# A gated FFN behind chunked attention: the zero columns beside h go, the centre tap comes first, and the hand-written order and engine tables are replaced

## The chip, the cores and the metric

The kernel runs on one core of one Trainium2 chip. The metric is device microseconds per execution, the median of three runs. The engines are written as in the profile: PE (TensorE, with PEld for its weight loads), DVE (VectorE), ACT (ScalarE), POOL (GpSimd) and SP (SyncE, which issues the DMAs here).

## The reference, cut to what matters

Chunked attention with 8 memory keys makes x (4 batches, 768 tokens, 512 channels). What the change touches is the second half:

```
h = relu(x @ w_in)                      # 768 tokens x 1024 channels, per batch
conv_out[t] = w0*h[t-1] + w1*h[t] + w2*h[t+1]    # per channel; h[-1] = h[768] = 0
out = (h * sigmoid(conv_out)) @ w_out   # 768 x 512
```

## The kernel before, in words

Channels lie on the 128 partitions and tokens along the free axis. h is made in 32 blocks: 4 batches of 8 channel blocks ("fc"), each 128 channels by 768 tokens, in two halves of 384 tokens. Attention is made in 32 pieces (batch, half, pair of heads).

Each float32 operand of a large product is split into a high and a low float32r part, and three products (high·high, high·low, low·high) replace one. The weights arrive as float64 words and are split on the chip by `from_f64`; one letter of W_IN, W_OUT, W_CONV for each block says how. For W_OUT, "C" scales the low part on ACT and multiplies on POOL, "M" does both in one DVE scalar_tensor_tensor; a lower-case letter puts the `max` of line 280 on POOL, not DVE.

One attention piece runs: scores on PE (L381), row maximum on DVE (L390), subtraction on DVE (L395) and one exp on ACT (L401) where SOFT has "V", or a small scaling on DVE (L407) and six exps with a bias on ACT (L413) where SOFT has "A"; row sum, reciprocal, normalisation (L427, on DVE or POOL by NORM), a transpose (TURN), the product with v on PE (L486), and the split of x into high (ACT, L489) and low (DVE, L492).

`ffn_in` makes one half of a block: 12 products on PE (L508) into one of four PSUM tiles "f", then the ReLU on ACT (L522) from "f" into h. h lives in a slot of the pool "u": 32 slots, 770 columns wide, which also hold x and the two parts of every gated block. Columns 0 and 769 of h must be zero for the convolution. The ReLU of the first half therefore issues a two-column memset on POOL (L521) ahead of itself, and waits for it.

`gated` then makes, for one block: the first tap (a scaling by a per-channel weight, on ACT, L534, or DVE, L538, by TAP), two scalar_tensor_tensor taps on DVE (L543), the sigmoid on ACT (L546), the multiplication by h (L550, on DVE or POOL by MULT; KEEP says whether the result goes over h or over the tap tile "w"), the high part (a copy on ACT, L554) and the low part (L557, on DVE or POOL by LO). `ffn_out` reads the parts of all 8 blocks of a batch: 24 products on PE (L569) for each 128 tokens. The last 128 tokens of batch 3 are done in two column halves.

The order is written out by hand. The program first lists 1529 operations (a product group, a ReLU, a tap and so on is one each), numbered as they are defined; `ORDER` then says in which order they are issued. Every engine executes its own operations in that order, one queue for each engine, and waits are made by what an operation reads and overwrites. Slots of a pool are handed out in that order as well: an operation that first writes a slot waits for the last readers of what was there.

Of the kernel before, what the change touches and what calls it, by code (L numbers as in the profile page):

```python
# [9 lines left out]
F32 = mybir.dt.float32  # L10
# [19 lines left out]
W_IN, W_OUT, W_CONV = "SMMSmMCM", "CMMMCMCM", "r"  # L30
TAP = "VAAAAAVAAAAAAAAAAAVVVVVAVVAAVAAA"
MULT = "VGGGGGGVGVGGGGGGVVGVGGGVGVGGVGGG"
LO = "VGGGVVGVGGGGVVGGVGVVGVGVVGVGVVVV"
SOFT = "AVVAAAAVVVAAVVVAVVVAVVVVVVAVVAVV"
NORM = "GGVVGVVGGGGGVGGGVVVGVVVVVGGGVGGV"
KEEP = "KKKKKNNKKKKKKNKKNKKNNKKNNNNNNKKK"
HOME = "wwwwwwwwwwwwwwwwwwwxwwwwwxxxwwxx"
# [158 lines left out]
def attention_then_gated_ffn(  # L196
# [302 lines left out]
    def ffn_in(b, fc, hf):  # L499
# [19 lines left out]
        def relu():  # L519
            if hf == 0:  # L520
                G.memset(h.t[:, 0 : S + 2 : S + 1], 0.0)  # L521
# [175 lines left out]
```

## Time and profile before

| | before |
|---|---|
| runs (three) | 366.35, 366.37, 367.98 us |
| median | 366.37 us |
| profiled execution, its own time | 366.92 us |
| its span, first to last instruction | 365.1 us |
| granted clock, mean | 0.995 |
| busy: PE, PEld, DVE, ACT, POOL | 339.9, 301.4, 252.0, 210.6, 104.6 us |

Busy times are those of the whole span. They average over stages with different limits, so the stages are read one by one below. Matmuls are pipelined, and a PE that is shown as busy can still be paced by others. POOL's spans are rough.

### The profile page before, as it was taken

What the parts mean: (1) busy time and instruction counts of PE and PEld (TensorE: products, weight loads), DVE (VectorE), ACT (ScalarE), POOL (GpSimd) and SP (SyncE); (2) the same over time, 40 slices, a digit from 0 to 9 for tenths busy, and PEclk for the clock granted to TensorE, in tenths of its full rate; (3) what the DMA queues carried; (4) which work ended last, traced back from release to release, by engine and by line L of the source; (5) the groups of instructions that cost most, each with busy time, mean ns of one, the idle gap of its engine ahead of it and who ended that gap; (6) DMA issues with size and microseconds to landing.
All of it is one profiled execution on the core that took longest, in us unless ns stands there. A gap on an engine that the chain in (4) does not pass through costs nothing.

```text
span 365.1 us, 7418 instructions
## 1 busy us (share of the span) xinstructions
PE 339.9 (93%) x2955; PEld 301.4 (83%) x2955; DVE 252.0 (69%) x429; ACT 210.6 (58%) x387; POOL 104.6 (29%) x114
## 2 busy tenths in 40 slices
PE   1799999899989988799999999899999999999996
PEld 1689899889979967779988789788998888888886
DVE  4999999999999999998999956230444991320000
ACT  2566879799889867857366795221566424420101
POOL 3314033284012353540316283400005615300000
PEclk9999999999999999899999999999999999999999
DMA  7997769467758372535054364411000102110102
GB/s 296 405 397 256 271 221 308 145 227 247 271 160 250 133 229 74 186 125 189 0 173 143 118 230 161 136 38 57 31 1 0 59 30 86 59 57 29 59 29 86
DMA packets 26386, 54.50 MB, mean 149 GB/s; under 512 B 3056, under 2 KB 13168, under 8 KB 26352
## 3 DMA queue, kind: packets, MB, share of 16 engines
q1 hardware_dynamic: 26352, 54.04, 42.6%
q8 instruction: 23, 0.38, 0.4%
q14 instruction: 11, 0.09, 0.1%
HBM read 44.79 MB, written 9.24 MB: 148 GB/s over the span
## 4 chain that ended last, share of the span: by engine, by line
PE 41%; DVE 21%; ACT 5%; issue 2%; DMA 1%; POOL 1%; SPq 0%; DVEq 0%; ACTq 0%; POOLq 0%
PE f L569 29%; PE f L508 10%; DVE w L543 9%; DVE w_top L293 2%; PE ta L486 1%; DVE e L427 1%; DVE z L422 1%; DVE u L492 1%; DVE top L390 1%; DVE u L557 1%; DMA w<-in_q_dram 1%; ACT u L522 1%; ACT e L413 1%; DVE w L457 1%; DVE e L395 1%
## 5 line engine op out<-in xcount | busy, mean ns | idle before, releaser
L508 PE MATMUL f<-u,w_in_hi 128*128 128x384 f32 x512 | 143.8, 347 | 6.2 <-ACT u L522 3.8
L569 PE MATMUL f<-w_out_hi,u 128*128 128x512 f32 (+1 forms) x400 | 125.2, 387 | 0.4 <-ACT w_top L580 0.4
L508 PEld LDWEIGHTS f<-u,w_in_hi 128*128 128x128 f32 x512 | 94.6, 190 | 10.4 <-ACT u L522 5.1
L569 PEld LDWEIGHTS f<-w_out_hi,u 128*128 128x128 f32 x400 | 74.1, 188 | 16.5 <-ACT w_top L580 0.8
L508 PE MATMUL f<-u,w_in_lo 128*128 128x384 f32 x256 | 87.2, 341 | 0.0
L543 DVE SCALAR_TENSOR_TENSOR w<-u,cw,w 128x768 f32<-128x768 f32 x64 | 78.1, 1231 | 4.4 <-ACT w L534 3.7
L569 PE MATMUL f<-w_out_lo,u 128*128 128x512 f32 (+1 forms) x200 | 77.1, 385 | 0.0
L522 ACT ACTIVATE u<-f 128x384 f32<-128x384 f32 x64 | 30.6, 493 | 35.1 <-PE f L508 27.7
L508 PEld LDWEIGHTS f<-u,w_in_lo 128*128 128x128 f32 x256 | 48.7, 190 | 0.6
L580 ACT COPY w_top<-f 128x512 f32<-128x512 f32 (+1 forms) x25 | 14.2, 572 | 59.8 <-PE f L569 54.0
L569 PEld LDWEIGHTS f<-w_out_lo,u 128*128 128x128 f32 x200 | 37.6, 188 | 7.2
L550 POOL TENSOR_TENSOR u<-w,u 128x768 f32<-128x768 f32 x16 | 28.9, 1810 | 41.5 <-ACT w L546 41.5
L546 ACT ACTIVATE w<-w 128x768 f32<-128x768 f32 x32 | 26.7, 845 | 15.8 <-DVE w L543 14.3
L486 PEld LDWEIGHTS ta<-a_d,w 128*64 128x64 f32 x768 | 26.1, 146 | 6.8 <-ACT a_d L446 3.3
L486 PE MATMUL ta<-a_d,w 128*64 128x64 f32 x768 | 28.9, 232 | 2.7 <-ACT a_d L446 1.8
L427 POOL TENSOR_TENSOR e<-e,z 128x384 f32<-128x384 f32 x17 | 16.1, 951 | 53.2 <-DVE z L424 46.6
L492 DVE TENSOR_TENSOR u<-ta,u 128x384 fp32r<-128x384 f32 x32 | 17.5, 548 | 12.8 <-ACT u L489 12.7
L381 PE MATMUL s<-k,w 128*64 128x64 f32 x672 | 24.8, 227 | 0.6 <-DVE e L395 0.6
L381 PEld LDWEIGHTS s<-k,w 128*64 128x64 f32 x672 | 22.1, 141 | 3.7 <-issue 2.0
L390 DVE TENSOR_REDUCE top<-s 128x6 f32<-128x384 f32 x32 | 17.2, 539 | 9.6 <-PE s L381 9.6
L557 DVE TENSOR_TENSOR u<-u,u 128x768 fp32r<-128x768 f32 x9 | 9.4, 1058 | 20.7 <-PE f L569 10.0
L557 POOL TENSOR_TENSOR u<-u,u 128x768 fp32r<-128x768 f32 x11 | 21.5, 1955 | 5.4 <-ACT u L554 3.5
(63 smaller groups left out, 373.7 us busy)
## 6 DMA issues: line engine op xcount, KB each, us to landing
w<-in_v_dram SPq DMA_DIRECT2D x32, 384.0 KB, 4.4
w<-in_q_dram SPq DMA_DIRECT2D x28, 384.0 KB, 4.3
k<-in_k_dram SPq DMA_DIRECT2D x28, 252.0 KB, 4.5
out_dram<-w_top SPq DMA_DIRECT2D x23, 256.0 KB, 2.0
w<-in_w_in_dram SPq DMA_DIRECT2D x8, 512.0 KB, 6.7
w<-in_w_out_dram SPq DMA_DIRECT2D x8, 512.0 KB, 4.6
t_dram<-w SPq DMA_DIRECT2D x15, 192.0 KB, 2.0
a_d<-t_dram SPq DMA_DIRECT2D x30, 96.0 KB, 2.5
```

What stands on the lines that cost most here:

```text
L381: nc.tensor.matmul(s.t[j * D : (j + 1) * D, o : o + KW], lhsT=q_[:, c], rhs=k_t.t[:, c * STEP : c * STEP + KW], start=True, stop=True,)
L390: lambda: V.tensor_reduce(out=pairs(top.t), in_=s_(), axis=AX.X, op=ALU.max), (s,), (top,),
L427: lambda: (V if norm == "V" else G).tensor_tensor(out=keys(e), in0=keys(e), in1=pairs(z.t).unsqueeze(3).broadcast_to([P, NG, 2, KW]), op=A ...
L486: nc.tensor.matmul(y, lhsT=v_g[:, g, u, h], rhs=a_d.t[:, :, o], start=True, stop=True)
L492: lambda: V.tensor_tensor(out=x.t[:, TW:S], in0=a.t[:, :TW], in1=x.t[:, :TW].bitcast(F32), op=ALU.subtract), (a, (x, 0)), ((x, 1),),
L508: nc.tensor.matmul(f.t[:, :TW], lhsT=w_in_p[c][:, fc, cc], rhs=x.t[:, a * TW : (a + 1) * TW], start=(cc == 0 and i == 0), stop=(cc == NCC ...
L522: A.activation(h.t[:, o : o + TW], f.t[:, :TW], AF.Relu)
L543: lambda j=j: V.scalar_tensor_tensor(out=c.t, in0=at(j), scalar=w[j], in1=c.t, op0=ALU.mult, op1=ALU.add),
L546: plan.op("A", act(S), lambda: A.activation(c.t, c.t, AF.Sigmoid), (c,), (c,), table="sigmoid")
L550: lambda: (V if mult == "V" else G).tensor_tensor(out=y_(), in0=c.t, in1=at(1), op=ALU.mult), (c, h), (y,), shared=True,
L557: lambda: (V if lo == "V" else G).tensor_tensor(out=g_lo(), in0=y_(), in1=g_hi().bitcast(F32), op=ALU.subtract),
L569: nc.tensor.matmul(ps.t[:, :n], lhsT=gs[b, fc][a].t[:, tt * P : (tt + 1) * P], rhs=w_out_p[c][:, fc, o : o + n], start=(fc == 0 and i == 0 ...
```

## The change

Four things change in the code.

- A "u" slot is 768 columns wide. h has no zero columns, and the ReLU issues no memset.
- The first tap is the centre one, over all 768 columns. The two outer taps are added over 767 columns each: the left one reads columns 0 to 766 of h and adds into columns 1 to 767 of the tap tile; the right one reads 1 to 767 and adds into 0 to 766. The count of instructions is the same.
- The engine tables and `ORDER` are new. Before to after, operations on DVE: TAP 10 to 5 of 32 (the rest on ACT), MULT 9 to 14, LO 17 to 17 with 12 blocks that trade places, SOFT "V" 21 to 19, NORM 15 to 16. For the weights of the output product one block goes from C to M (6) and one from M to m (1); the small conv weights go from r to R. KEEP trades four blocks, and HOME puts two more v tiles into another pool. TURN and W_IN are the same.
- Two cost figures that the order was planned with (`less=-15` lines, 75 to 185; -10 to -20) change; they issue nothing. The scratch for dynamic DMAs is 2048 bytes, before 1024.

```diff
-W_IN, W_OUT, W_CONV = "SMMSmMCM", "CMMMCMCM", "r"
-TAP = "VAAAAAVAAAAAAAAAAAVVVVVAVVAAVAAA"
-MULT = "VGGGGGGVGVGGGGGGVVGVGGGVGVGGVGGG"
-LO = "VGGGVVGVGGGGVVGGVGVVGVGVVGVGVVVV"
-SOFT = "AVVAAAAVVVAAVVVAVVVAVVVVVVAVVAVV"
-NORM = "GGVVGVVGGGGGVGGGVVVGVVVVVGGGVGGV"
-KEEP = "KKKKKNNKKKKKKNKKNKKNNKKNNNNNNKKK"
-HOME = "wwwwwwwwwwwwwwwwwwwxwwwwwxxxwwxx"
+W_IN, W_OUT, W_CONV = "SMMSmMCM", "CmMMCMMM", "R"
+TAP = "AAAAAAVAAAAAAAAAAVAVAVAAVAAAAAAA"
+MULT = "VGGVGGGGGVGGGGGGVVGVVVVVVGVGVVGG"
+LO = "VGGVVVVVVVGGGGVGVVVGGVGVVGGGGVVG"
+SOFT = "AVVAAAAVAVVAVVVAVVVAVVVVVVAAAVAV"
+NORM = "GGVVGGVGGGGGVGGGVVVGVVVVVGVGVVGV"
+KEEP = "KKKKKNNKKKKKKNKKNKKNNKKNKNKNNNNK"
+HOME = "wwwwwwwwwwwwwwwwwwxxwwwwwxxxwxxx"
 ORDER = [
...
-    plan.pool("u", [lambda t, i=i: work.tile([P, S + 2], t, name=f"u{i}", tag=f"u{i}", bufs=1) for i in range(NU)])
+    plan.pool("u", [lambda t, i=i: work.tile([P, S], t, name=f"u{i}", tag=f"u{i}", bufs=1) for i in range(NU)])
...
-        o = 1 + hf * TW
-
-        def relu():
-            if hf == 0:
-                G.memset(h.t[:, 0 : S + 2 : S + 1], 0.0)
-            A.activation(h.t[:, o : o + TW], f.t[:, :TW], AF.Relu)
-
-        plan.op("A", act(TW, True), relu, (f,), ((h, hf),))
+        plan.op(
+            "A", act(TW, True), lambda: A.activation(h.t[:, hf * TW : (hf + 1) * TW], f.t[:, :TW], AF.Relu), (f,), ((h, hf),)
+        )
...
-            plan.op("A", act(S, ptr=1), lambda: A.activation(c.t, at(0), AF.Copy, scale=w[0]), H, (c,))
+            plan.op("A", act(S, ptr=1), lambda: A.activation(c.t, h.t, AF.Copy, scale=w[1]), H, (c,))
...
-        for j in (1, 2):
+        for j, to, at in ((0, slice(1, S), slice(0, S - 1)), (2, slice(0, S - 1), slice(1, S))):
             plan.op(
                 "V", vec(S, 1, 1),
-                lambda j=j: V.scalar_tensor_tensor(out=c.t, in0=at(j), scalar=w[j], in1=c.t, op0=ALU.mult, op1=ALU.add),
-                (*H, c), (c,), shared=True,
+                lambda j=j, to=to, at=at: V.scalar_tensor_tensor(
+                    out=c.t[:, to], in0=h.t[:, at], scalar=w[j], in1=c.t[:, to], op0=ALU.mult, op1=ALU.add
+                ), (*H, c), (c,), shared=True,
             )
...
-    nc = _bacc.Bacc("TRN2", target_bir_lowering=False, num_devices=1, dynamic_dma_scratch_size=1024)
+    nc = _bacc.Bacc("TRN2", target_bir_lowering=False, num_devices=1, dynamic_dma_scratch_size=2048)
```

The new `ORDER` has 1528 entries, one less, since a C block has one operation more than an M block. Read as operations it is close to the old one: the same attention pieces and product groups come in nearly the same sequence on PE, and the activation tables are switched 20 times in both. Two places of it matter below:

| counted in `ORDER` | before | after |
|---|---|---|
| ahead of batch 3's first product group, on DVE: MULT, TAP, L395, L407 | 7, 7, 19, 10 | 8, 4, 17, 12 |
| there on DVE, weights: max of 512 columns, scalar_tensor_tensor, conv max | 15, 42, 0 | 14, 43, 1 |
| there on POOL: LO, MULT | 6, 16 | 4, 14 |
| there on ACT: taps | 17 | 20 |
| still to come on PE from there: L569 products, groups of L508, transposes | 414 + 48 half, 64, 0 | 417 + 48 half, 64, 1 |
| L569 products to come when batch 3's last block is first read | 108 + 48 half (fc 7) | 141 + 48 half (fc 7), 150 + 48 half (fc 4) |
| last low parts of batch 3 on the engine that makes them | fc 5, fc 7 on DVE | fc 3, fc 1, fc 4 on POOL, one after the other |

## Rows read from the trace of the kernel before

**Rows 1.** The page's busy times: us, share of the span, count.
```profile
PE 339.9 (93%) x2955; PEld 301.4 (83%) x2955; DVE 252.0 (69%) x429; ACT 210.6 (58%) x387; POOL 104.6 (29%) x114
```

**Rows 2.** Stages: length, busy us of PE, PEld, DVE, ACT, POOL, PEclk, DMA.
```profile
60.00:135.00 75.00, 70.28 (x815) 65.49 (x815) 72.94 (x122) 64.67 (x110) 25.77 (x26) 1.00 0.65 215
135.00:150.00 15.00, 11.34 (x110) 10.49 (x107) 14.67 (x23) 10.77 (x16) 5.21 (x6) 0.95 0.44 137
...
165.00:225.00 60.00, 59.65 (x550) 51.94 (x547) 53.50 (x84) 40.93 (x67) 23.26 (x13) 1.00 0.44 146
...
285.00:300.00 15.00, 15.00 (x66) 12.14 (x65) 14.96 (x13) 4.82 (x7) 6.10 (x3) 1.00 0.10 37
```

**Rows 3.** The chain that ended last, from 226 us: start, us, what.
```profile
228.12 1.61 POOL u L557
...
229.82 0.15 POOL u L521 x2
229.97 0.49 ACT u L522
...
230.50 5.01 PE f L508 x27
...
272.82 89.23 PE f L569 x408
```

**Rows 4.** PE's timeline, its longest wait after the start: [idle before <-releaser].
```profile
147.94 0.55 PE L439 MATMUL ta<-ident,e 128*128 128x128 f32 x3 [2.14 <-DVE e L427]
...
230.50 0.44 PE L508 MATMUL f<-u,w_in_hi 128*128 128x384 f32 x1 [1.59 <-ACT u L522]
```

**Rows 5.** The view of waits: us in total, times, longest.
```profile
ACT u L522 <- POOL u L521: 7.2, 5, 3.4
...
PE f L508 <- ACT u L522: 3.8, 4, 1.6
```

**Rows 6.** Groups by line: busy us, mean ns of one, idle before.
```profile
L543 DVE SCALAR_TENSOR_TENSOR w<-u,cw,w 128x768 f32<-128x768 f32 x64 | 78.1, 1231 | 4.4 <-ACT w L534 3.7
...
L550 POOL TENSOR_TENSOR u<-w,u 128x768 f32<-128x768 f32 x16 | 28.9, 1810 | 41.5 <-ACT w L546 41.5
...
L557 POOL TENSOR_TENSOR u<-u,u 128x768 fp32r<-128x768 f32 x11 | 21.5, 1955 | 5.4 <-ACT u L554 3.5 <-PE f L508 1.0 <-PE f L569 0.7
L534 ACT ACTIVATE w<-u,cw 128x768 f32<-128x768 f32 x22 | 20.7, 939 | 0.8 <-ACT u L489 0.3
...
L395 DVE TENSOR_TENSOR e<-s,top 128x384 f32<-128x384 f32 x21 | 11.5, 551 | 0.3
L427 DVE TENSOR_TENSOR e<-e,z 128x384 f32<-128x384 f32 x15 | 11.0, 736 | 0.2
...
L280 DVE TENSOR_SCALAR w_top<-w_top 128x512 f32<-128x512 f32 x15 | 6.6, 443 | 5.4 <-ACT w_top L276 5.4
...
L407 DVE TENSOR_SCALAR top<-top 128x6 f32<-128x6 f32 x11 | 3.6, 329 | 0.1
L348 DVE SCALAR_TENSOR_TENSOR w_out_lo<-w 128x512 fp32r<-128x512 uint32 x5 | 3.4, 688 | 0.1
...
L591 DVE TENSOR_TENSOR cw<-cw_hi,cw_lo 128x24 f32<-128x24 f32 x1 | 0.2, 175 | 0.0
```

**Rows 7.** Single lines: ns min/median/max, first and last start; L543 of 115 to 124 us.
```profile
L538 DVE TENSOR_SCALAR w<-u,cw x10: 578/612/1406, 60.6 to 292.7; 128x768 f32<-128x768 f32 x10
...
L550 DVE TENSOR_TENSOR w<-w,u x5: 951/1583/2300, 174.8 to 314.8; 128x768 f32<-128x768 f32 x5
L550 DVE TENSOR_TENSOR u<-w,u x4: 923/951/1535, 68.4 to 192.0; 128x768 f32<-128x768 f32 x4
...
L543 DVE SCALAR_TENSOR_TENSOR w<-u,cw,w x6: 1007/1012/1019, 114.5 to 123.3; 128x768 f32<-128x768 f32 x6
```

**Rows 8.** Timelines of DVE and POOL, from 280 us.
```profile
285.32 7.41 DVE L543 SCALAR_TENSOR_TENSOR w<-u,cw,w 128x768 f32<-128x768 f32 x3
...
324.21 1.83 DVE L557 TENSOR_TENSOR u<-u,u 128x768 fp32r<-128x768 f32 x2 [7.07 <-PE f L569]
```

More of the change, by code (lines that the diff above doesn't have):

```diff
@@ L418, in attention @@
         else:
-            plan.op("V", 75, lambda: V.memset(e.t[D:, NG - 1, 1 + 2 * KW - RIGHT : 1 + 2 * KW], 0.0), (), (e,), less=-15)
+            plan.op("V", 185, lambda: V.memset(e.t[D:, NG - 1, 1 + 2 * KW - RIGHT : 1 + 2 * KW], 0.0), (), (e,), less=-15)
         plan.op(
@@ L449, in place @@
                     )
-                plan.op("A", 480, place, (t,), ((a_d, p),), less=-10)
+                plan.op("A", 480, place, (t,), ((a_d, p),), less=-20)
         else:
@@ L530, in gated @@
         w = [cw[:, 3 * fc + j : 3 * fc + j + 1] for j in range(3)]
-        at = lambda j: h.t[:, j : j + S]
         H = ((h, 0), (h, 1), "cw")
         if tap == "A":
-            plan.op("A", act(S, ptr=1), lambda: A.activation(c.t, at(0), AF.Copy, scale=w[0]), H, (c,))
+            plan.op("A", act(S, ptr=1), lambda: A.activation(c.t, h.t, AF.Copy, scale=w[1]), H, (c,))
         else:
@@ L537, in gated @@
                 "V", vec(S, 2, 1),
-                lambda: V.tensor_scalar(out=c.t, in0=at(0), scalar1=w[0], scalar2=None, op0=ALU.mult), H, (c,), shared=True,
+                lambda: V.tensor_scalar(out=c.t, in0=h.t, scalar1=w[1], scalar2=None, op0=ALU.mult), H, (c,), shared=True,
             )
-        for j in (1, 2):
+        for j, to, at in ((0, slice(1, S), slice(0, S - 1)), (2, slice(0, S - 1), slice(1, S))):
             plan.op(
                 "V", vec(S, 1, 1),
-                lambda j=j: V.scalar_tensor_tensor(out=c.t, in0=at(j), scalar=w[j], in1=c.t, op0=ALU.mult, op1=ALU.add),
-                (*H, c), (c,), shared=True,
+                lambda j=j, to=to, at=at: V.scalar_tensor_tensor(
+                    out=c.t[:, to], in0=h.t[:, at], scalar=w[j], in1=c.t[:, to], op0=ALU.mult, op1=ALU.add
+                ), (*H, c), (c,), shared=True,
             )
         plan.op("A", act(S), lambda: A.activation(c.t, c.t, AF.Sigmoid), (c,), (c,), table="sigmoid")
-        y, y_ = (h, lambda: at(1)) if keep == "K" else (c, lambda: c.t)
+        y = h if keep == "K" else c
         plan.op(
             mult, vec(S) if mult == "V" else 2.0 * S,
-            lambda: (V if mult == "V" else G).tensor_tensor(out=y_(), in0=c.t, in1=at(1), op=ALU.mult), (c, h), (y,), shared=True,
+            lambda: (V if mult == "V" else G).tensor_tensor(out=y.t, in0=c.t, in1=h.t, op=ALU.mult), (c, h), (y,), shared=True,
         )
         g = gs[b, fc] = [Tile("u", dtype=F32R) for _ in range(2)]
-        g_hi, g_lo = (lambda x=x: x.t[:, :S] for x in g)
-        plan.op("A", act(S), lambda: A.copy(out=g_hi(), in_=y_()), (y,), (g[0],))
+        g_hi, g_lo = g
+        plan.op("A", act(S), lambda: A.copy(out=g_hi.t, in_=y.t), (y,), (g[0],))
         plan.op(
             lo, vec(S) if lo == "V" else 2.4 * S,
-            lambda: (V if lo == "V" else G).tensor_tensor(out=g_lo(), in0=y_(), in1=g_hi().bitcast(F32), op=ALU.subtract),
+            lambda: (V if lo == "V" else G).tensor_tensor(out=g_lo.t, in0=y.t, in1=g_hi.t.bitcast(F32), op=ALU.subtract),
             (y, g[0]), (g[1],), shared=True,
```

136 rows, old and new, of the table ORDER are left out of this document.

## The prediction

> **What bounds the kernel now.** I read the busy times first. PE is busy for 339.9 us of the span of 365.1 [rows 1], so the end can only come earlier by what PE loses to waits and to slow pacing. The stages come second: from 60 to 225 us DVE is nearly full (72.94 of 75 us, 14.67 of 15, 53.50 of 60) while PE has holes, and at 135 to 150 us PE is down to 11.34 of 15 with a granted clock of 0.95 [rows 2]. Third, the chain that ended last: behind 230.50 us it is PE alone, product after product, with 89.23 us of output products as its last piece; ahead of it the chain runs over other engines [rows 3]. So there are two stages. Up to some 230 us DVE's queue decides how far PE gets; from there PE has all it needs. A microsecond that is taken from DVE's queue ahead of this handover moves the end; one taken behind it does not.
>
> Fourth, how the handover happens. POOL makes a low part for 1.61 us, then two memsets for the zero columns of h, then ACT runs the ReLU that waited for them, then PE goes on [rows 3]. PE stood for 1.59 us there, its second longest wait after the start; the longest is 2.14 us at 147.94, behind a normalisation on DVE [rows 4]. The view of waits has the same place from ACT's side: the ReLU waited for the memset 5 times, 7.2 us in all, 3.4 us at most, and PE waited for a ReLU 4 times, 3.8 us in all [rows 5]. The memset itself is nothing; it stands in POOL's queue behind work that has nothing to do with this h.
>
> **The change, part by part.** The sum is made for the handover, by the counts of the table in the section on the change.
>
> *The memset.* Without it the ReLU waits for its product and its slot alone. The wait of 1.59 us [rows 4] should go: -1.6 us. The bounds are 0, if the slot or DVE makes PE wait there instead, and -3.8, if every wait of PE for a ReLU goes [rows 5]. I take the 1.6, since it is the only one of these that the chain shows right ahead of PE's unbroken run.
>
> *The taps over 767 columns.* One column in 768 of 1.0 us is about 1.3 ns, 64 times: 0.1 us, taken as nothing. Odd starts are a rival below.
>
> *DVE's own work ahead of the handover.* One multiplication more at 951 ns, three scalings fewer at 612 [rows 7]; two subtractions fewer at 551, two small scalings more at 329; one scalar_tensor_tensor of weights more at 688, one max fewer at 443, the conv max as the 175 of its nearest row [rows 6]. That is 0.95 - 1.84 - 1.10 + 0.66 + 0.69 - 0.44 + 0.18 = -0.9 us. Moves between blocks within the stage, LO's above all, do not change the sum.
>
> *DVE slowed by POOL.* A tap takes 1007 to 1019 ns in a quiet stretch [rows 7], 1231 on average [rows 6], and three of them 7.41 us where POOL is at work [rows 8]. The multiplications by h on DVE say the same: 951 at the lowest, 1583 in the middle [rows 7]. So fewer POOL operations make DVE faster. Ahead of the handover two low parts (1955 ns) and two multiplications (1810) leave POOL [rows 6]: 7.5 us. The price for each: the taps lost 64 x 0.22 = 14.0 us and the normalisations 15 x (0.736 - 0.551) = 2.8, for 104.6 us of POOL [rows 1, 6], 0.16 each. So -1.2 us. Bounds: 0, if the moved work never met a tap, and 0.72 each, from 285 to 300 us (7.41 less 3 x 1.01 lost, for 6.10 us of POOL [rows 2, 8]): -5.4 us. I take the average, as it is over the whole kernel.
>
> *PE's own work.* The new order leaves 3 more output products and one more transposition group behind the handover. 408 of the last products, 48 of them half as wide, take 89.23 us [rows 3], 0.232 for a full one; a group of three transposes takes at most 0.55 [rows 4]. So +1.2 us.
>
> *ACT.* Three taps more at 939 ns [rows 6] are 2.8 us. They hide behind DVE: ACT is busy for 40.93 of the 60 us from 165 to 225 [rows 2]. From 60 to 135 us it is 64.67 of 75, so there the cover is thinner. Without cover it would be +2.8.
>
> *Slots, DMAs, scratch, cost figures.* Narrower slots, the second weight block's max on POOL, two v tiles in another pool and the scratch change no instruction that the chain waits for. The queue of SP holds the same loads in nearly the same sequence. All taken as nothing.
>
> *Behind the handover.* PE is full. The gated blocks of batch 3 must be ready when PE reads them. Before, the last low part ended at 326.04 us [rows 8]; PE's last product ended at 362.05, and with 108 full and 48 half products to come (30.6 us) it read that block first at 331.4. That is 5.4 us of cover. After, PE reads the last of these blocks with 150 full ones to come, 9.7 us earlier. So the cover is gone unless those blocks are ready earlier. They can be: the last two low parts of before waited 7.07 us for PE to free a slot [rows 8], and the new order gives the last ones the slots of batch 3's own h. I take +0.
>
> Sum: -1.6 - 0.9 - 1.2 + 1.2 = -2.5 us. Span 365.1 - 2.5 = 362.6; the profiled execution's own 366.92 gives 364.4. The median shown, 366.37, is 0.55 below that execution, so the prediction is 363.9 us.
>
> **A rule against the change.** The row first: of the taps of before, one of each pair reads h from an odd column and one from an even one, and six in a row, three of each kind, took 1007, 1012 and 1019 ns at the least, the middle and the most [rows 7]. The multiplication that writes over h, at an odd column, has the same 951 as the one that writes the tap tile from column 0 at its least [rows 7]. So an odd start costs nothing that shows. The Trainium skill, "Vector Engine (DVE) Microarchitecture Reference", section "Measured stream behaviour on trn2", says that a port streams fully only for runs that begin on an 8-byte boundary, and gives 1.30 ns a column for pairs that start on an odd word against 1.054. Read as a rule for a whole tap, that would be an estimate of 0.19 us for each of the taps, some 9 us ahead of the handover. By that rule the two halves of these six would have to differ; the trace disagrees, as long runs from an odd word go at full rate.
>
> **The rivals.**
>
> *A, nothing comes of it.* PE's wait at the handover returns under another name (DVE, or the slot) and the POOL operations that leave did not touch taps. Then -0.9 + 1.2 = +0.3: 366.7 us. For it: DVE stays full up to the handover, and a new order of 1528 entries makes waits of its own. Against: the chain names POOL at the handover, not DVE.
>
> *B, more than forecast.* The work that leaves POOL is what collided with taps: -1.6 - 0.9 - 5.4 + 1.2 = -6.7, 359.7 us; half way to it, 361.8. For it: PE's hole of 2.14 us and the clock of 0.95 lie in the full stage [rows 2, 4]. Against: from 165 to 225 us DVE has 6.5 us idle already.
>
> *C, slower: batch 3's last block is late.* The last three low parts stand one behind the other in POOL's queue. If the last block is made no sooner than before, 326.04 less the 2.5, at 323.5, PE would want it at 331.4 - 9.7 - 2.5 = 319.2. It waits 4.3 us, and 1.0 more as POOL takes 1.955 for a low part [rows 6], where a two-input operation on DVE takes 0.95 [rows 7]: 363.9 + 5.3 = 369.2 us. It decides for slower once the last low part ends later than some 323.5 us. Against: POOL is busy for 6.10 us in the 15 from 285 [rows 2], and the old delay was one for slots.
>
> *D, odd starts cost a little.* At most the spread above, 12 ns for each of 64 taps: +0.8, 364.7 us.
>
> **How the numbers follow.** Forecast (362.0 to 364.5) 0.45; B 0.12; A 0.25; D 0.03; C 0.15. About 0.5%, 1.8 us, is what a measurement of this kernel can tell from no change, so the bounds are 364.5 and 368.2. Faster is the forecast and B, 0.57; the same A and D, 0.28; slower C, 0.15. The range takes B's half way with a margin at the low end and A with one at the high end, 360.3 to 367.8; it leaves out C and B's far end, under 2 in 10.
>
> **What would show it.** In the profile of the changed kernel: no POOL memset in the ReLU's line and no wait of it for POOL; PE without a hole of over 1 us between 220 and 232 us; the last unbroken run of PE beginning some 2 us earlier; the mean tap under 1231 ns, POOL at some 90 us, DVE within 3 us of 252; no wait of L569 for a low part behind 300 us. Wrong if PE waits for POOL or DVE in the last 60 us (C), or if the handover lies where it was with another releaser (A).

## The result, and the profile after

After the change the median is 362.48 us (362.43 to 362.65, three runs) against 366.37: a ratio of 0.9881, interval [0.984, 0.9921]. The profiled execution takes 362.65 us with a span of 360.9, 4.2 us less than the span before. In the changed file the ReLU is L518, the first tap L528 (ACT) and L532 (DVE), the outer taps L537, the sigmoid L541, the multiplication L545, the high part L549, the low part L552 and the output products L564.

The page's busy times, which answer to [rows 1]:

```profile
PE 339.0 (94%) x2955; PEld 299.6 (83%) x2955; DVE 255.5 (71%) x431; ACT 215.5 (60%) x401; POOL 100.4 (28%) x75
```

The stages, which answer to [rows 2], with two more:

```profile
60.00:135.00 75.00, 70.42 (x839) 65.21 (x839) 73.90 (x120) 64.14 (x111) 30.13 (x17) 1.00 0.66 214
135.00:150.00 15.00, 11.73 (x90) 10.33 (x85) 14.61 (x21) 11.14 (x17) 6.78 (x3) 1.00 0.57 187
150.00:165.00 15.00, 14.81 (x147) 13.35 (x148) 14.57 (x29) 9.67 (x20) 5.23 (x3) 0.89 0.46 158
165.00:225.00 60.00, 60.00 (x516) 52.73 (x515) 49.28 (x87) 42.94 (x75) 12.73 (x8) 1.00 0.41 134
225.00:231.00 6.00, 6.00 (x34) 5.75 (x33) 2.37 (x4) 1.49 (x4) 0.00 (x0) 1.00 0.48 158
...
285.00:300.00 15.00, 15.00 (x66) 12.09 (x65) 15.00 (x8) 6.58 (x10) 14.32 (x6) 1.00 0.19 70
```

The same two more stages of before:

```profile
150.00:165.00 15.00, 14.15 (x116) 12.27 (x116) 14.54 (x26) 9.78 (x19) 7.40 (x9) 0.94 0.35 119
...
225.00:231.00 6.00, 4.41 (x26) 4.09 (x25) 2.43 (x8) 2.56 (x10) 3.45 (x5) 1.00 0.66 207
```

PE's longest waits on its timeline, its waits by releaser, and the chain that ended last, which answer to [rows 4], [rows 5] and [rows 3]:

```profile
130.65 0.62 PE L508 MATMUL f<-u,w_in_hi 128*128 128x384 f32 x2 [1.81 <-DVE u L492]
...
150.19 0.69 PE L508 MATMUL f<-u,w_in_hi 128*128 128x384 f32 x1 [1.38 <-ACT u L518]
```

```profile
PE f L508 <- DVE u L492: 3.1, 3, 1.8
PE f L508 <- ACT u L518: 1.4, 1, 1.4
```

```profile
150.19 4.95 PE f L508 x18
...
269.50 88.28 PE f L564 x402
```

The ReLU no longer waits for POOL, and the hole of 1.59 us at 230 us is gone. More than that: PE's last hole lies at 150 us, and from 165 to 225 us it is busy throughout. The last piece of output products ends at 269.50 + 88.28 = 357.78 us, before at 362.05 [rows 3]; it starts 3.3 us earlier and has six products fewer to do, so the whole gain is there by some 270 us. Of the 4.2 us, 3.3 are idle time of PE that is gone: 1.6 at the hole of 230 us and 1.7 in the stages up to 225 us. The other 0.9 us is PE's busy time, 339.0 for 339.9.

Two things don't fit the forecast. They stand in the groups by line, which answer to [rows 6], and in the single lines, which answer to [rows 7] (least, middle and most ns):

```profile
L537 DVE SCALAR_TENSOR_TENSOR w<-u,cw,w 128x767 f32<-128x767 f32 x64 | 80.6, 1268 | 4.1 <-ACT w L528 3.3
L545 POOL TENSOR_TENSOR u<-w,u 128x768 f32<-128x768 f32 x12 | 26.0, 2166 | 61.3 <-ACT w L541 59.4 <-DMA k<-in_k_dram 1.8
...
L552 POOL TENSOR_TENSOR u<-u,u 128x768 fp32r<-128x768 f32 x9 | 19.2, 2143 | 15.5 <-ACT u L549 14.1 <-PE f L564 1.4
```

```profile
L545 POOL TENSOR_TENSOR u<-w,u x12: 1832/2064/2685, 68.0 to 274.6; 128x768 f32<-128x768 f32 x12
...
L545 POOL TENSOR_TENSOR w<-w,u x6: 1831/2155/2577, 78.8 to 298.2; 128x768 f32<-128x768 f32 x6
```

The taps became slower, 1268 ns for 1231 [rows 6]. And one POOL multiplication takes 2166 ns on average for 1810 [rows 6]; its least time is 1.83 us. The same single line of before has 1544 ns:

```profile
L550 POOL TENSOR_TENSOR u<-w,u x16: 1544/1688/2312, 62.4 to 314.8; 128x768 f32<-128x768 f32 x16
```

The operation itself is the same; but h, its second input, now begins at column 0 of its slot, as the tap tile does. The experiments had to settle what that costs, and what the order brings.

### The profile page after: what moved, and what is told of

Its sections match the earlier page's. It is cut to its first block, busy times and chain, and to the rows that moved or that the text cites. A ratio compares the mean times of both kernels' runs of the same rounds, so it can differ in the third digit from the quotient of the medians.

```text
span 360.9 us, 7378 instructions
## 1 busy us (share of the span) xinstructions
PE 339.0 (94%) x2955; PEld 299.6 (83%) x2955; DVE 255.5 (71%) x431; ACT 215.5 (60%) x401; POOL 100.4 (28%) x75
## 4 chain that ended last, share of the span: by engine, by line
PE 58%; DVE 22%; issue 2%; ACT 2%; POOL 0%; ACTq 0%; POOLq 0%; DVEq 0%
PE f L564 38%; PE f L508 16%; DVE w L537 9%; PE ta L486 2%; PE s L381 2%; DVE u L492 1%; DVE top L390 1%; DVE z L422 1%; DVE e L395 1%; DVE e L427 1%; DVE w L457 1%; DVE u L545 1%; DVE w L306 1%; DVE w L301 1%; DVE w_top L286 1%
## 5 line engine op out<-in xcount | busy, mean ns | idle before, releaser
L508 PE MATMUL f<-u,w_in_hi 128*128 128x384 f32 x512 | 143.9, 347 | 4.6 <-DVE u L492 3.1
L564 PE MATMUL f<-w_out_hi,u 128*128 128x512 f32 (+1 forms) x400 | 125.7, 388 | 0.0
L508 PEld LDWEIGHTS f<-u,w_in_hi 128*128 128x128 f32 x512 | 94.0, 190 | 9.9 <-DVE u L492 5.0
L564 PEld LDWEIGHTS f<-w_out_hi,u 128*128 128x128 f32 x400 | 74.1, 188 | 16.0
L508 PE MATMUL f<-u,w_in_lo 128*128 128x384 f32 x256 | 86.8, 339 | 0.0
L537 DVE SCALAR_TENSOR_TENSOR w<-u,cw,w 128x767 f32<-128x767 f32 x64 | 80.6, 1268 | 4.1 <-ACT w L528 3.3
L564 PE MATMUL f<-w_out_lo,u 128*128 128x512 f32 (+1 forms) x200 | 77.2, 386 | 0.0
L508 PEld LDWEIGHTS f<-u,w_in_lo 128*128 128x128 f32 x256 | 48.7, 190 | 0.7
L518 ACT ACTIVATE u<-f 128x384 f32<-128x384 f32 x64 | 30.6, 491 | 23.7 <-PE f L508 23.6
L564 PEld LDWEIGHTS f<-w_out_lo,u 128*128 128x128 f32 x200 | 37.6, 188 | 7.3
L545 POOL TENSOR_TENSOR u<-w,u 128x768 f32<-128x768 f32 x12 | 26.0, 2166 | 61.3 <-ACT w L541 59.4
L541 ACT ACTIVATE w<-w 128x768 f32<-128x768 f32 x32 | 26.9, 844 | 16.2 <-DVE w L537 16.1
L486 PEld LDWEIGHTS ta<-a_d,w 128*64 128x64 f32 x768 | 24.9, 140 | 5.6 <-ACT a_d L446 2.2
L486 PE MATMUL ta<-a_d,w 128*64 128x64 f32 x768 | 27.7, 227 | 1.9 <-ACT a_d L446 1.0
L427 POOL TENSOR_TENSOR e<-e,z 128x384 f32<-128x384 f32 x16 | 15.3, 958 | 45.8 <-DVE z L424 38.3
L528 ACT ACTIVATE w<-u,cw 128x768 f32<-128x768 f32 x27 | 25.3, 937 | 3.7 <-PE s L381 2.1
L545 POOL TENSOR_TENSOR w<-w,u 128x768 f32<-128x768 f32 x6 | 13.1, 2188 | 40.0 <-ACT w L541 40.0
L552 POOL TENSOR_TENSOR u<-u,u 128x768 fp32r<-128x768 f32 x9 | 19.2, 2143 | 15.5 <-ACT u L549 14.1
```

What stands on the lines that cost most here:

```text
L427: lambda: (V if norm == "V" else G).tensor_tensor(out=keys(e), in0=keys(e), in1=pairs(z.t).unsqueeze(3).broadcast_to([P, NG, 2, KW]), op=A ...
L486: nc.tensor.matmul(y, lhsT=v_g[:, g, u, h], rhs=a_d.t[:, :, o], start=True, stop=True)
L508: nc.tensor.matmul(f.t[:, :TW], lhsT=w_in_p[c][:, fc, cc], rhs=x.t[:, a * TW : (a + 1) * TW], start=(cc == 0 and i == 0), stop=(cc == NCC ...
L518: "A", act(TW, True), lambda: A.activation(h.t[:, hf * TW : (hf + 1) * TW], f.t[:, :TW], AF.Relu), (f,), ((h, hf),)
L528: plan.op("A", act(S, ptr=1), lambda: A.activation(c.t, h.t, AF.Copy, scale=w[1]), H, (c,))
L537: lambda j=j, to=to, at=at: V.scalar_tensor_tensor(out=c.t[:, to], in0=h.t[:, at], scalar=w[j], in1=c.t[:, to], op0=ALU.mult, op1=ALU.add) ...
```

## The experiments

Twelve kernels ran. They ran in three sets, each on one chip beside the kernel before, whose median was 367.23 us in the first set (e1 to e4), 367.2 in the second (e5 to e7, m1) and 367.53 in the third (e8 to e10, m2). The kernel after did not run again in these sets, so a comparison with its 362.48 us goes across sets; e6 and e9 stand where it stands. m1 and m2 ran once each. "Narrow" is the code of the change without its order: no memset, centre tap first, outer taps over 767 columns.

| kernel | order and tables | h starts at column | median us (range, runs) | ratio to before |
|---|---|---|---|---|
| e1 | old | 0, narrow | 367.85 (367.21 to 368.78, 12) | 1.0008 [0.9984, 1.0031] |
| e2 | new | 1, with memset | 360.26 (359.96 to 360.44, 5) | 0.9805 [0.978, 0.9831] |
| e3 | new, MULT and LO old | 0, narrow | 366.47 (366.16 to 367.16, 12) | 0.9976 [0.996, 0.9991] |
| e4 | old, MULT and LO new | 0, narrow | 368.29 (367.06 to 369.21, 12) | 1.0014 [0.9991, 1.0036] |
| e5 | new | 1, narrow | 359.76 (359.14 to 360.46, 6) | 0.9787 [0.9757, 0.9817] |
| e6 | new | 8, narrow | 362.53 (361.61 to 363.0, 6) | 0.9856 [0.9828, 0.9885] |
| e7 | old | 1, narrow | 363.67 (362.58 to 364.4, 6) | 0.9892 [0.9862, 0.9921] |
| e8 | new | 1 in batches 0, 1; 0 in 2, 3 | 359.77 (359.64 to 359.86, 5) | 0.9786 [0.9755, 0.9818] |
| e9 | new | 0 in batches 0, 1; 1 in 2, 3 | 362.39 (362.25 to 363.23, 5) | 0.9863 [0.983, 0.9896] |
| e10 | new | 1; high part of g at 2 | 359.05 (358.94 to 360.96, 6) | 0.9776 [0.9741, 0.9812] |

The granted clock doesn't sort these. At 0.999 to 1.0, e9 takes 362.25 to 362.39 us and e8 359.64 to 359.86. Within one kernel a lower clock can go with up to 1 us more: e9's two runs at 0.99 and 0.991 take 362.8 and 363.23.

### e1 and e2: the two halves of the change

e1 is the kernel before with the narrow code; e2 is the kernel after with the ReLU, taps, slots and scratch (1024 bytes) of before.

```diff
 # e1, against before (order and tables kept)
-    plan.pool("u", [lambda t, i=i: work.tile([P, S + 2], t, name=f"u{i}", tag=f"u{i}", bufs=1) for i in range(NU)])
+    plan.pool("u", [lambda t, i=i: work.tile([P, S], t, name=f"u{i}", tag=f"u{i}", bufs=1) for i in range(NU)])
...
-                G.memset(h.t[:, 0 : S + 2 : S + 1], 0.0)
...
-        for j in (1, 2):
+        for j, to, at in ((0, slice(1, S), slice(0, S - 1)), (2, slice(0, S - 1), slice(1, S))):
```

> The kernel before with one part of the change: h 768 columns wide, no memset, centre tap first, outer taps over 767 columns; order and engine tables as before. Theory (the terms of my sum): only the wait for the memset goes, so PE's hole of 1.59 us at 230.5 us is gone and the time is 1.6 us less, some 364.8 us. Rival 1: the wait returns under another name, because DVE's queue is late at the same place: 366.4 us, unchanged within 0.5 us. Rival 2: every wait of PE for a ReLU goes, up to 3.8 us less, 362.6 us, which would be the whole gain of the change.

> The changed kernel with the other part taken back: slots of 770 columns, the POOL memset in front of each first ReLU, the old taps; order and engine tables are the new ones, the scratch is 1024. Theory: the order and the tables bring what the memset does not, some 2.3 of the 3.9 us, so 364.1 us, and waits of the ReLU for POOL come back. Rival 1: the new order gains nothing without the narrow h (its POOL queue was laid out without memsets): 366 us or more. Rival 2: the memset costs nothing in the new order, since POOL stands behind nothing there: 362.5 us.

Neither time was expected, and no rival named what follows. The narrow code alone brings nothing, and the order and tables alone bring 7.0 us, more than the whole change. The hole at 230 us is gone in e1 too, so the memset's wait was removed; something else took the time back. e1's groups and its longest PE wait:

```profile
L537 DVE SCALAR_TENSOR_TENSOR w<-u,cw,w 128x767 f32<-128x767 f32 x64 | 81.8, 1289 | 4.3 <-ACT w L528 3.6
L545 POOL TENSOR_TENSOR u<-w,u 128x768 f32<-128x768 f32 x16 | 34.6, 2166 | 37.9 <-ACT w L541 37.9
```

```profile
149.68 0.55 PE L439 MATMUL ta<-ident,e 128*128 128x128 f32 x3 [2.81 <-DVE e L427]
```

The same 16 POOL multiplications take 34.6 us for 28.9 [rows 6], taps 1289 ns for 1231, and PE's hole behind DVE at 148 us grows from 2.14 [rows 4] to 2.81. e1's PE also does less in the first 30 us (17.34 us of work for 19.39), waiting for the first loads; that is not the reason, since e4, with the same narrow code, starts as before (19.27) and is no faster. In e2, with h at column 1, the multiplication is back at 1.54 us:

```profile
L550 POOL TENSOR_TENSOR u<-w,u x12: 1542/1554/2310, 68.9 to 272.7; 128x768 f32<-128x768 f32 x12
```

The ReLU of e2 still waits for the memset, but PE waits no longer for a ReLU than in e5 (1.5 us in all, there 2.1):

```profile
ACT u L522 <- POOL u L521: 5.5, 4, 1.6
```

### e3 and e4: order without its split, split without its order

```diff
 # e3, against after; e4 makes the reverse exchange in e1
-MULT = "VGGVGGGGGVGGGGGGVVGVVVVVVGVGVVGG"
-LO = "VGGVVVVVVVGGGGVGVVVGGVGVVGGGGVVG"
+MULT = "VGGGGGGVGVGGGGGGVVGVGGGVGVGGVGGG"
+LO = "VGGGVVGVGGGGVVGGVGVVGVGVVGVGVVVV"
```

> The changed kernel with MULT and LO of before: the same new order, but five multiplications go back to POOL and the low parts lie as before. Theory of the prediction (fewer POOL operations ahead of the handover speed DVE by 1.2 us and cost it 0.9 less with the rest): 1 to 2 us slower than the changed kernel, 363.5 to 364.5 us. Rival: the profile after shows the taps ahead of 231 us no faster than before (58.3 us for 48, before 57.8), so the split between DVE and POOL does nothing by itself: within 0.5 us of 362.5.

> The kernel before with the narrow h and with MULT and LO of the changed kernel; the order is the old one. Theory: as the narrow h alone, less 1 us for the POOL work that leaves: 363.8 us. Rival: equal to the narrow h alone within 0.5 us, or slower, since the old order gave these operations no room on DVE: 365 to 367 us.

With the old split the new order gives 4.0 us back (366.47 against 362.48); in the old order the new split gives nothing (368.29 against 367.85). They belong together: e3 is 2 us slower than its theory had it, and for e4 the rival, no change, holds. e3's busy times, and then three of its lines on DVE and two of the same in the kernel after:

```profile
PE 339.5 (93%) x2955; PEld 299.0 (82%) x2955; DVE 259.3 (71%) x426; ACT 215.3 (59%) x401; POOL 109.5 (30%) x80
```

```profile
L537 DVE SCALAR_TENSOR_TENSOR w<-u,cw,w 128x767 f32<-128x767 f32 x64 | 78.4, 1234 | 4.1 <-ACT w L528 3.3
L427 DVE TENSOR_TENSOR e<-e,z 128x384 f32<-128x384 f32 x16 | 13.8, 863 | 0.3
...
L532 DVE TENSOR_SCALAR w<-u,cw 128x768 f32<-128x768 f32 x5 | 6.4, 1290 | 2.6 <-POOL u L552 1.8 <-ACT u L518 0.8
```

```profile
L427 DVE TENSOR_TENSOR e<-e,z 128x384 f32<-128x384 f32 x16 | 10.6, 665 | 0.3
...
L532 DVE TENSOR_SCALAR w<-u,cw 128x768 f32<-128x768 f32 x5 | 3.3, 651 | 0.5 <-ACT u L518 0.5
```

From e3 to after DVE takes over five multiplications, 4.8 us at 951 ns [rows 7], and yet its busy time falls, from 259.3 to 255.5. So the old split had slowed DVE by some 8.6 us. The taps are not what it slowed: they take 1234 ns in e3 and 1268 in the kernel after. The normalisations and the first taps on DVE are, 3.2 and 3.1 us of it. In the old order the same exchange relieves DVE of less: from e1 to e4 its busy time rises from 254.4 to 258.0, 3.6 us for 4.8 of added work, though there the taps do get faster, 1289 to 1223 ns. And not all of the 4.0 us lies ahead of 231 us: in e3 output products wait 1.1 us for low parts of DVE between 285 and 330 us, which they don't in the kernel after. Which of MULT and LO does how much was not tried.

### m1: the operations by themselves

m1 leaves all of the reference out: POOL multiplications, subtractions and DVE taps over 768 columns, alone and side by side.

```diff
+        G.tensor_tensor(out=at(y, 0), in0=at(c, 0), in1=at(h, 0), op=ALU.mult)   # L30; L32: h from 1, L34: 2, L36: 4, L38: 8
...
+        tap(0)    # six alone, three of them tap(1), in L27; then 16 beside 8 of POOL, h from 0 (L57) and from 1 (L64)
```

> A kernel of its own that leaves all of the reference out: POOL multiplications of 128 x 768 float32 with nothing beside them, the second input 0, 1, 2, 4 and 8 columns off the first, the output 0 and 1 off, then subtractions into float32r, taps on DVE alone with an even and an odd start, and 8 multiplications on POOL beside 16 taps on DVE, once with equal starts and once one column off. Theory: 1.83 us at offsets 0 and 8, 1.54 at 1; taps 1.0 us alone at any start; beside taps both engines take longer, and DVE loses less to the POOL work that is one column off. Rival: all offsets cost 1.54 or 1.83 alike here, and the difference in the kernels is made by what runs beside them.

Groups by line, and then the timeline of the taps alone and beside POOL:

```profile
L30 POOL TENSOR_TENSOR y<-c,h 128x768 f32<-128x768 f32 x3 | 5.4, 1799 | 5.5 <-DMA c<-in_q_dram 5.4
L36 POOL TENSOR_TENSOR y<-c,h 128x768 f32<-128x768 f32 x3 | 5.4, 1799 | 0.2
L34 POOL TENSOR_TENSOR y<-c,h 128x768 f32<-128x768 f32 x3 | 4.6, 1545 | 0.2
...
L32 POOL TENSOR_TENSOR y<-c,h 128x768 f32<-128x768 f32 x3 | 4.6, 1542 | 0.2
```

```profile
55.03 6.29 DVE L27 SCALAR_TENSOR_TENSOR d<-a,w,d 128x768 f32<-128x768 f32 x6
...
66.50 19.89 POOL L57 TENSOR_TENSOR y<-c,h 128x768 f32<-128x768 f32 x8
67.45 28.19 DVE L27 SCALAR_TENSOR_TENSOR d<-a,w,d 128x768 f32<-128x768 f32 x16
...
98.66 17.83 POOL L64 TENSOR_TENSOR y<-c,h 128x768 f32<-128x768 f32 x8
99.61 26.13 DVE L27 SCALAR_TENSOR_TENSOR d<-a,w,d 128x768 f32<-128x768 f32 x16
```

The second input's start decides POOL's time: 1.80 us from column 0 or 4, 1.54 from 1 or 2. The taps don't care: six alone take 6.29 us, half of them reading from column 1. And the two engines nearly take turns. Sixteen taps alone would take 16 x 6.29 / 6 = 16.8 us; beside eight POOL multiplications they take 28.19 or 26.13. When POOL ends at 86.39, 9.25 us of taps are left, so DVE has finished some seven taps beside eight POOL operations. (Three taps took 7.41 us beside POOL in the kernel before [rows 8], 2.5 each; the slowest here takes 2.44.) Each POOL operation thus costs DVE (28.19 - 16.8) / 8 = 1.4 us, or 1.2 with unlike starts. The difference, 2.06 / 8 = 0.26 us, is just what the operation itself is longer by.

The Trainium skill, "SBUF — State Buffer", section "SBUF: two separate sides", says that a DVE operation with two SBUF inputs and a GpSimd operation that reads SBUF exclude each other for the whole of the instruction. The trace agrees in the main, though a POOL operation beside taps grows by 0.60 us (a middle of 2395 ns for 1799), not by the whole 1.02 of a tap.

### e5, e6, e7: only the start of h

e5 is the kernel after with h from column 1 on; e6 has it from column 8 in the same slots; e7 is e5's code in the old order.

```diff
 # e5, against after
+OFF = 1     # e6: 8
...
-    plan.pool("u", [lambda t, i=i: work.tile([P, S], t, name=f"u{i}", tag=f"u{i}", bufs=1) for i in range(NU)])
+    plan.pool("u", [lambda t, i=i: work.tile([P, S + 8], t, name=f"u{i}", tag=f"u{i}", bufs=1) for i in range(NU)])
...
-            "A", act(TW, True), lambda: A.activation(h.t[:, hf * TW : (hf + 1) * TW], f.t[:, :TW], AF.Relu), (f,), ((h, hf),)
+            "A", act(TW, True), lambda: A.activation(h.t[:, OFF + hf * TW : OFF + (hf + 1) * TW], f.t[:, :TW], AF.Relu), (f,), ((h, hf),)
...
+        hv = lambda: h.t[:, OFF : OFF + S]     # read in place of h.t by taps, multiplication, high and low part
```

> The changed kernel with h stored from column 1 of a slot of 776 columns, still without zero columns or memset, same order and tables, scratch 1024. In the runs so far the POOL multiplication by h takes 1.54 us at the least where h lies at column 1 and 1.83 us where it lies at column 0, alike the tap tile it is multiplied with. Theory (the place of h prices the POOL multiplication): the 1.54 us come back, and the time is that of the new order with the old h, 360.3 us, or less. Rival 1 (the memset, or what waits for it, is what made the old h faster here): 362.5 us. Rival 2 (the pitch of the slots or the scratch): 360.3 us here and in the run with h at column 8 as well.

> The same with h from column 8, 32 bytes into the slot: same pitch and scratch as the run with h at column 1. Theory (the place of h prices the POOL multiplication, and 32 bytes count as alike): 1.83 us for a multiplication and 362.5 us. Rival 2 (pitch or scratch): 360.3 us. If the multiplication takes 1.54 us here, any offset counts.

> The kernel before with its order and tables, h at column 1, no zero columns, no memset, outer taps over 767 columns: the memset alone is taken away. Theory (my term for the memset holds, and was eaten in the run with h at column 0 by slower POOL multiplications): 1.6 us less than before, 364.8 to 365.6 us beside 366.4 to 367.2. Rival: the wait is absorbed anyway: as before within 0.5 us.

The single line of e5 and of e6, and e5's taps:

```profile
L548 POOL TENSOR_TENSOR u<-w,u x12: 1544/1734/2376, 67.9 to 271.4; 128x768 f32<-128x768 f32 x12
```

```profile
L548 POOL TENSOR_TENSOR u<-w,u x12: 1817/2034/2664, 69.1 to 275.2; 128x768 f32<-128x768 f32 x12
```

```profile
L539 DVE SCALAR_TENSOR_TENSOR w<-u,cw,w 128x767 f32<-128x767 f32 x64 | 77.8, 1224 | 4.4 <-ACT w L530 3.6
```

e6 stands where the kernel after stands (362.53 for 362.48), so neither the slots' width nor the scratch (1024 bytes in e6, 2048 there) is it. e5 is 2.8 us faster than e6, and only the start of h differs, column 1 for column 8. ACT's work on h is the same in both: 492 and 490 ns for a ReLU, 938 for a first tap. In the old order the start is worth 367.85 - 363.67 = 4.2 us (e1 against e7). And the narrow code without its price, before against e7, brings 3.5 us, more than the 1.6 that e7 was expected to bring.

### e8 and e9: where the price is paid

```diff
 # e8, against e5
-OFF = 1
+off = lambda b: 1 if b < 2 else 0     # e9: b >= 2
...
-        hv = lambda: h.t[:, OFF : OFF + S]
+        hv = lambda: h.t[:, off(b) : off(b) + S]
```

> The kernel after, with h stored from column 1 on for batches 0 and 1 only; batches 2 and 3 keep h at column 0. Theory (POOL's multiplication takes 1.80 us instead of 1.54 us where h and the tap tile start alike, and this costs time where DVE is full, up to some 165 us): most of the 2.7 us between the kernel after (362.48) and h at column 1 throughout (359.76) comes, 359.9 to 360.7 us. Rival 1 (the price is paid evenly, by every multiplication): half of it, 361.1 us. Rival 2 (the price is paid in the later batches alone): no change, 362.5 us. POOL's multiplications of batches 0 and 1 show a minimum of 1.54 us, those of batches 2 and 3 one of 1.83 us.

> The counterpart: h stored from column 1 on for batches 2 and 3 only, column 0 for batches 0 and 1. Theory (early price): 362.0 to 362.5 us, little or nothing of the 2.7 us. Rival 1 (even price): 361.1 us. Rival 2 (late price): 359.8 us.

All of it in batches 0 and 1: e8 equals e5, e9 equals the kernel after. The stage from 60 to 165 us, of e8 and then of e9:

```profile
60.00:165.00 105.00, 98.53 (x1083) 89.83 (x1082) 102.10 (x175) 85.99 (x148) 38.61 (x23) 1.00 0.64 202
```

```profile
60.00:165.00 105.00, 96.48 (x1073) 88.04 (x1071) 103.07 (x170) 85.34 (x146) 42.02 (x23) 1.00 0.65 202
```

DVE is full in both. In e8 it starts 175 operations for 170, PE 1083 for 1073, and POOL needs 38.61 us for the same 23 operations that take 42.02 in e9. MULT gives POOL 13 multiplications in batches 0 and 1 in either order; 13 x 0.26 = 3.4 us is what they lose by themselves, and 2.6 us is found between e8 and e9. The 4.2 us of the old order are more than that; where they are paid was not tried. Of batches 2 and 3 the longer multiplications cost nothing: from 165 us on PE has no hole in e8, though they are the slow ones there.

### m2: which starts

m2 leaves all of the reference out as well: POOL operations alone, with other pairs of start columns.

```diff
+        G.tensor_tensor(out=at(y, 0), in0=at(c, 0), in1=at(h, 3), op=ALU.mult)   # L33: 0 and 3; L41: 1 and 0; L45: 3 and 0; L47: 1 and 2
...
+        G.tensor_tensor(out=at(r, 0), in0=at(c, 1), in1=at(h, 0), op=ALU.subtract)   # L51: 1 and 0; L53: 1 and 2
```

> Leaves all of the reference out: single POOL multiplications of 768 columns and subtractions, each alone, with the two inputs at chosen start columns. Theory (only the distance of the two inputs' start columns counts, by its remainder over 4 columns, which is 16 bytes): inputs 1, 2, 5 or 6 columns apart take 1.54 us, 4 or 8 apart or equal 1.80 us, 3 and 7 apart not known (1.54 or 1.80). Inputs at 1 and 2 take 1.54 us like 0 and 1; at 1 and 0 likewise if the distance alone counts. Rival (the second input's own start counts, not the distance): first input at 1, 2 or 3 with the second at 0 takes 1.80 us. VectorE's two-input operation takes the same time at 0/0 and 0/1.

```profile
L33 POOL TENSOR_TENSOR y<-c,h 128x768 f32<-128x768 f32 x3 | 5.4, 1801 | 5.7 <-DMA c<-in_q_dram 5.5
L41 POOL TENSOR_TENSOR y<-c,h 128x768 f32<-128x768 f32 x3 | 5.4, 1796 | 0.2
L51 POOL TENSOR_TENSOR r<-c,h 128x768 fp32r<-128x768 f32 x3 | 5.4, 1795 | 0.2
...
L45 POOL TENSOR_TENSOR y<-c,h 128x768 f32<-128x768 f32 x3 | 4.6, 1542 | 0.2
...
L47 POOL TENSOR_TENSOR y<-c,h 128x768 f32<-128x768 f32 x3 | 4.6, 1542 | 0.2
L53 POOL TENSOR_TENSOR r<-c,h 128x768 fp32r<-128x768 f32 x3 | 4.6, 1542 | 0.2
...
L60 DVE TENSOR_TENSOR y<-c,h 128x768 f32<-128x768 f32 x3 | 2.9, 959 | 0.1
L58 DVE TENSOR_TENSOR y<-c,y 128x768 f32<-128x768 f32 x3 | 2.9, 958 | 0.1
```

The nine pairs of starts here and the six of m1 all fit one rule: the start of the second input less that of the first, taken modulo 4 columns, gives 1.54 us for 1 or 2 and 1.80 for 0 or 3. So the sign counts: first at 1 and second at 0 (L41, L51) is slow. Neither the theory, by which the distance alone counts, nor the rival, by which the second start alone does, had this. That is how the low part of before stands (h from 1, the high part from 0), with 1815 ns at its least. A two-input operation on DVE takes 958 ns with the second input from column 0 (L58) and 959 from column 1 (L60).

### e10: the low part too

```diff
 # e10, against e5
-OFF = 1
+OFF, HI = 1, 2      # the high part of g is written, and read by PE, from column 2 on
...
-        g_hi, g_lo = (lambda x=x: x.t[:, :S] for x in g)
+        g_hi, g_lo = lambda: g[0].t[:, HI : HI + S], lambda: g[1].t[:, :S]
```

> h from column 1 on throughout (359.76 us) and the high part of g stored from column 2 on, so that POOL's subtraction for the low part reads inputs that start unlike too. Theory: the subtraction falls from some 1.84 us to 1.54 us, POOL's sum falls by some 2 us, and the time by 0 to 1 us, 358.8 to 359.8 us, since part of the low parts lies beside taps. Rival 1 (the low parts are hidden altogether): 359.8 us, no change. Rival 2 (TensorE loads the high parts from column 2 more slowly): over 360.3 us.

```profile
L555 POOL TENSOR_TENSOR u<-u,u x9: 1542/1735/2281, 149.5 to 291.3; 128x768 fp32r<-128x768 f32 x9
...
L555 POOL TENSOR_TENSOR u<-w,u x6: 1545/1604/2176, 207.9 to 308.9; 128x768 fp32r<-128x768 f32 x6
```

```profile
PE 337.4 (94%) x2955; PEld 297.9 (83%) x2955; DVE 247.2 (69%) x431; ACT 215.5 (60%) x401; POOL 89.8 (25%) x75
```

The subtraction falls to 1.54 us too, and POOL's sum from 94.6 us in e5 to 89.8. The median is 359.05 us, 0.7 under e8 of the same set, though one of its six runs took 360.96. That one run is also the one at a clock of 0.995, the others show 1.0. Rival 2 is out by the time, and PE's weight loads of these parts take 188 ns in e5 and e10 alike. e10 is the fastest version measured, faster than both given kernels; five of its six runs lie below all of e8's.

## Why the number was right, and its steps were not

The forecast was 363.9 us and the time is 362.48: the right direction, inside the range and inside the bounds of the forecast's own case. But that the sum arrived there is luck: a gain that was taken too small and a loss that was not seen cancel for the most part.

**The memset, -1.6.** The mechanism is as described: no wait of the ReLU for POOL, no hole at 230 us. The size holds for neither order. In the old order the narrow code with h left at column 1 (e7) brings 3.5 us, near the bound of 3.8 that stood beside it. In the new order, e2 against e5, it brings 0.5 us, within what the intervals leave open: the ReLU of e2 waits 5.5 us for the memset, but PE doesn't wait for it the longer. The term was read in the old order and added to a new one, as if the two were independent.

**The taps over 767 columns, 0, and "Slots, DMAs, scratch, cost figures … All taken as nothing".** This is the step that failed by omission. Slot width and scratch are nothing (e6), and a tap costs the same with h at column 0 or 1 (m1). But the change moves h by one column, and the reader of h that pays is POOL's multiplication, which no step costed: 1.80 us in place of 1.54, worth 2.8 us in the new order and 4.2 in the old.

**DVE slowed by POOL, -1.2.** The sign of the price was right, its size was not. The step took 0.16 us for each us of POOL, "the average, as it is over the whole kernel". Beside a DVE that is full, m1 measures (28.19 - 16.8) / 19.89 = 0.57 on average, near the upper bound of 0.72, and all of what a POOL operation grows by. The average of the whole kernel holds POOL work that met no tap. The forecast signs failed: the mean tap is 1268 ns, where under 1231 was forecast, POOL is at 100.4 us, not some 90, and DVE at 255.5, not within 3 us of 252. With h at column 1 the same order has taps at 1224 ns, POOL at 94.6 and DVE at 251.1 (e5), so much of this is the longer multiplication. The relief by the new split is seen between e3 and after, but on normalisations and first taps, not on the outer taps that the step was worked out from. In the old order it is some 1.2 us (e4).

**DVE's own work, -0.9, and PE's, +1.2.** They weren't measured apart. The order and tables together were forecast at -0.9 - 1.2 + 1.2 = -0.9. They bring 7.0 us with the old h (e2), 3.9 from e7 to e5, and 5.4 from e1 to after. Rival B had this: with the upper bound of POOL's price it has -5.1 for the same three terms. What in the order gives the rest is open beyond e3 and e4, which show that it needs the new MULT and LO.

**The handover.** The prediction had the last unbroken run of PE begin some 2 us earlier than 230. In after, PE has no hole past 150.19 us, so the second stage begins far earlier. Less is gained by that than it seems: from 150 to 225 us PE was idle for only 1.2 us before. The hole at 230 us is the largest single piece of idle time that went, 1.6 of 3.3 us; e1 lost it too and was no faster, e7 lost it and gained 3.5, so what it is worth is seen only with the start of h.

**ACT, 0, and behind the handover, 0.** Both hold as far as the waits show. PE waits once for a ReLU, 1.4 us; no output product waits for a low part. That settles C for this kernel; with the old MULT and LO in the same order low parts do come late, by 1.1 us, on DVE (e3). Batch 3's low parts do stand among the taps there: from 285 to 300 us DVE is busy for 15.00 us and POOL for 14.32, and PE doesn't notice.

**The rivals and the rule.** A is out. Of the two values of B, 361.8 lies nearer to the result than the forecast. Of its reason, that the work which leaves POOL is what collided with taps, e3 and m1 bear out a part: the work that left had slowed DVE, but other operations than the outer taps. What kept the result from B's far end is the start of h (e5, without that price, has 359.76). D is out: taps that read one input from an odd column cost nothing, in m1 as in [rows 7]. In e5 one tap of each pair has both inputs at odd columns, and such a pair takes 2.06 us at 113.53 us; so an odd start costs these long runs nothing, as the prediction had it. (The prediction's 951 ns for the multiplication that writes over h is the middle of that row; its least is 923 [rows 7]. Nothing hangs on it.) The start of a run did matter in this change, but on POOL, and between its two inputs.

In sum, against the median of before: order, tables and narrow code with h at column 1, -7.4 in the second set (e5); h at column 0, +2.8 (e6 against e5). That is -4.7, against -3.9 between the two medians shown; the kernel before stood 0.8 us higher in that set.

## What to carry to other kernels

When an edit moves a tile by a column, go through every reader of it, those on the engines that the edit isn't about too, and compare the least time of each line before and after. Price POOL work by the stage it stands in: side by side with taps each two-input POOL operation cost more DVE time (1.4 or 1.2 us in m1) than the 0.95 us that DVE would need for it; where PE had no hole to lose by, a longer one cost nothing (batches 2 and 3 of e8). In the kernel it depends on what the order puts beside it: the same exchange relieved DVE of 8.6 us in one order and of 1.2 in the other. Don't add up a wait read in one order with the gain of another.

## What the runs showed of the hardware

- A POOL operation with two float32 inputs of 768 columns takes 1.54 or 1.80 us, by the distance of the two starts: second less first, modulo 4 columns (16 bytes), 1 or 2 is fast, 0 or 3 slow (15 pairs of starts in m1 and m2, one execution each, and the low part in e10). Where the output starts doesn't matter: one column off, it stays at 1802 ns (m1). Why is open; only the time was measured.
- Two-input DVE operations and POOL nearly take turns: some seven taps of 1.02 us each beside eight POOL operations, whose middle rises from 1799 to 2395 ns, or from 1542 to 2138 (m1).
